# A chunked recurrence on one core: the 32 x 32 block inverse split into two halves of 16, masks back on VectorE, and a new table of lengths for the planner

## The chip, the cores and the metric

The kernel runs on one core of a Trainium2 chip. The metric is the device time of one execution in microseconds, as a median of several runs; lower is better. Engines are named as the profile does: PE is TensorE, DVE is VectorE, ACT is ScalarE, POOL is GpSimd, SP is SyncE, which here only issues transfers.

## What is computed

Three stages follow each other: a linear recurrence over 768 time steps in 4 x 8 heads of 40 dimensions, a mixture of eight experts with a capacity, and a dense feed-forward. The change lies in the first.

```python
for t in range(S):
    y[:, :, t] = np.einsum('bhd,bhde->bhe', rt, state)
    Sa = np.einsum('bhde,bhe->bhd', state, at)
    state_decay = state * wt[:, :, None, :] - np.einsum('bhd,bhe->bhde', Sa, bt)
    state = state_decay + np.einsum('bhd,bhe->bhde', vt, kt)
...
x = _moe_ref(x=x, **moe_kwargs)
return _moe2_ref(x=x, **moe2_kwargs)
```

## The kernel before

**Chunks.** Time is cut into 24 chunks of 32 steps. Within a chunk the dependence of a step on the steps before it is a lower triangular 32 x 32 matrix per head; its inverse turns 32 sequential updates into a few matmuls. Four chunks make one of six blocks (i = 0 to 5). A block has 8 steps of work, s = 8i to 8i + 7, each for one chunk and one half of the heads (hf).

**A step.** `kbt` transposes the keys (L531) into NI and Z, `chain` carries the state: X from AE and MV (L561), U from the inverse TB and X (L572), the new state MV from NI and MV (L589), scaled on VectorE (L593). `output` transposes MV into Z (L609), forms a product that is masked into RE (L622, L630), and sums the result into py (L641). After the last step of a chunk the router reads py.

**Preparation of a block.** `load` fetches, `prep` makes decays with two scans on VectorE (L370, L374), scales AE on VectorE or POOL (L377) and KB on POOL (L380). `gram` multiplies KB and AE (L407); one part of the product goes through the tile mab to DRAM (Md), the other is masked back into AE. `inverse` reads Md as Mu, one 32 x 32 matrix per partition, and eliminates column by column: a product into tmp (L470) and a subtraction from Tt (L472) for each of 30 columns, cut by rows into three ranges, two on VectorE (`VROW = (5, 10)`) and one on POOL. Tt goes to DRAM as Td and comes back as TB in the layout that `chain` needs.

**The first block.** `inverse_first` inverts two 16 x 16 halves on VectorE only, one instruction per half, column and operation (28 products, 28 subtractions). The off-diagonal quarter is then made on TensorE in `fix`: 32 small matmuls TB by Rt (L495), a masked copy to Wm (L497), 32 matmuls Wm by TB (L504), a copy back into TB. Rt is the transposed upper half, through DRAM as Tad.

**Masks.** With `GM = (0, 2)` half of AE's masks are a plain copy on ScalarE and a product on POOL (L431); the other half is one product on VectorE from PSUM (L422). `PM = 1` does the same for a quarter of RE's masks (L636 on POOL).

**What sets the order.** Nothing runs in the order of the code. `Sched` collects all operations of the recurrence with their lengths, dependences and due times (`when`, from START, STEP and the D constants), simulates the engines, picks the engine where several are allowed (`{'V': .., 'A': ..}`), and writes each engine's instructions in the order that it found. Where it expects TensorE to be idle it inserts small filler matmuls into py (L740). At run time each engine works through its list in that order, and so does SP's queue of transfers.

```python
NMV, NRE, NNI, NZ, NWT = 6, 7, 2, 3, 6
VROW = (5, 10)
START, STEP = 56.922, 7.975
DPREP, DINV, DOUT, DTURN = (-0.45, -0.74, 0.01, 1.52), (0.71, 9.76), 1.713, 0.084
EZ = 'A'
PM, ZM = 1, 0
GM = (0, 2)
```

Of the kernel before, what the change touches and what calls it, by code (L numbers as in the profile page):

```python
# [6 lines left out]
F32 = mybir.dt.float32  # L7
# [19 lines left out]
class Sched:  # L27
# [5 lines left out]
    AFTER = {'T': .25, 'V': .13, 'A': .18, 'P': .19, 'S': 0.}  # L33
# [198 lines left out]
    SLACK, PATIENCE, ALPHA = 0.021, 49.646, 0.109  # L232
# [3 lines left out]
SLACK0, LD0, LDS, PR0, PRS, LATEW, RV0, ZR0, ZRS, GR = 0.244, 0.0, 3.0, 18.956, 0.418, 0, 40.584, 52.618, 7.65, 1  # L236
# [39 lines left out]
def attention(ctx, tc, I, R, eng):  # L276
# [33 lines left out]
    TB4 = cp.tile([128, 2, 2, 8, 32], F32, name="TB")  # L310
    TBs = [TB4[:, m // 2, m % 2] for m in range(4)]
# [19 lines left out]
    Tad = dr.tile([32, 4, 16, 16], F32, name="Tad")  # L331
# [32 lines left out]
    def prep(n, h):  # L364
# [5 lines left out]
        op('V', .62, lambda E: E.tensor_tensor_scan(W, Bw[:, 0:528], d1, 0.0, ALU.mult, ALU.add), [('w', hf, h), 'd1'], ['W'])  # L370
        op('V', .07, lambda E: E.tensor_copy(WC, Ws[:, :, :, 32]), ['W'], [('WC', a, h)])
        op('V', .17, lambda E: E.reciprocal(rC, WC), [('WC', a, h)], [('rC', hf, h)])
        op(alu(512, EQ if n > 1 else 'V'), 0, lambda E: E.tensor_tensor(Qg, Ws[:, :, :, 0:32], rC.unsqueeze(3).broadcast_to([128, 2, 8, 32]), ALU.mult), ['W', ('rC', hf, h)], [('Q', hf, h)])
        op('V', .62, lambda E: E.tensor_tensor_scan(Bw[:, 527::-1], Bw[:, 527::-1], d1[:, ::-1], 1.0, ALU.mult, ALU.add), ['d1'], [('w', hf, h)])  # L374
# [7 lines left out]
    def turn(n):  # L382
        hf = n % 2
        Wo = Wts[n % NWT].rearrange("x (q j) e -> x q j e", j=2)
        for h in range(2):
# [5 lines left out]
            k = op('T', .44, f, [('Q', hf, x) for x in range(2)], [('ps', len(Q.ops))], ring='tr', act=1024)  # L391
# [5 lines left out]
    def gram(n, g):  # L397
        i, hf = divmod(n, 2)
        a, c8 = n % 4, 4 * (g // 2) + 2 * hf + g % 2
        AE, KB, mab = AEs[a], KBs[a], mabs[n % 2]  # L400
# [32 lines left out]
    def inverse_first(i):  # L433

        dma(Mu, Mds[i % 2].rearrange("c u t s -> (c u) t s"), 1 << 19, [('Md', i % 2, c) for c in range(8)], ['Mu'])
        op('P', 1.47, lambda E: (E.affine_select(Tt, Mu, [[-1, 32], [1, 32]], ALU.is_gt, 0.0, base=0, channel_multiplier=0),
                                 E.memset(Tt.rearrange("u a b -> u (a b)")[:, 0:1024:33], -1.0)), ['Mu'], [('Tt', x) for x in range(3)])
        for x in range(2):
            for k in range(1, 15):
                m, o, c = 15 - k, 16 * x, 16 * x + k  # L440
                tv = tmps[x][:, 0:k * m].rearrange("u (a b) -> u a b", b=m)
                d = alu(k * m, EI)
                tt = Tt[:, o:o + k, c + 1:o + 16]
                op(d, 0, lambda E, tv=tv, k=k, o=o, c=c, m=m: E.tensor_tensor(tv, Mu[:, c:c + 1, c + 1:o + 16].broadcast_to([128, k, m]), Tt[:, o:o + k, c:c + 1].broadcast_to([128, k, m]), ALU.mult),
                   ['Mu', ('Tt', x)], [('tmp', x)])
                op(d, 0, lambda E, tv=tv, tt=tt: E.tensor_tensor(tt, tt, tv, ALU.subtract), [('tmp', x)], [('Tt', x)])
        op(ev(256), 0, lambda E: copy(E, Ta, Tt[:, 0:16, 0:16].rearrange("u a b -> u b a")), [('Tt', 0)], ['Ta'])
        dma(Tds[i % 2].rearrange("u q s t -> (u q) s t"), Tt, 1 << 19, [('Tt', x) for x in range(3)], [('Td', i % 2)], QI)
# [5 lines left out]
    def inverse(i):  # L454
# [988 lines left out]
```

## Time and profile before

| what | us |
|---|---|
| median of 3 runs | 1141.11 (1140.74 to 1142.37) |
| the profiled execution | 1129.84 |
| its span, first to last instruction | 1128.1 |
| busy in the span: PE, DVE, ACT, POOL | 973.5, 791.4, 605.1, 484.1 |
| start of the first and end of the last py group of the recurrence | 107.4, 526 |

The shares of the whole span (PE 86%, DVE 70%) mix three stages. Up to about 530 us the recurrence runs, with DVE in the page's slices at nine tenths for most of the time up to 440 us; from 560 us on the experts and the feed-forward run, with PE at nine tenths throughout. The profiled execution is 1.0% below the median of the runs.

### The profile page before, as it was taken

What the parts mean: (1) busy time and instruction counts of PE and PEld (TensorE: products, weight loads), DVE (VectorE), ACT (ScalarE), POOL (GpSimd) and SP (SyncE); (2) the same over time, 40 slices, a digit from 0 to 9 for tenths busy, and PEclk for the clock granted to TensorE, in tenths of its full rate; (3) what the DMA queues carried; (4) which work ended last, traced back from release to release, by engine and by line L of the source; (5) the groups of instructions that cost most, each with busy time, mean ns of one, the idle gap of its engine ahead of it and who ended that gap; (6) DMA issues with size and microseconds to landing.
All of it is one profiled execution on the core that took longest, in us unless ns stands there. A gap on an engine that the chain in (4) does not pass through costs nothing.

```text
span 1128.1 us, 32070 instructions
## 1 busy us (share of the span) xinstructions
PE 973.5 (86%) x13099; PEld 863.8 (77%) x13099; DVE 791.4 (70%) x1857; ACT 605.1 (54%) x1426; POOL 484.1 (43%) x575
## 2 busy tenths in 40 slices
PE   4566787868877877997799999999999999999997
PEld 3555676756656666776688888999989999999997
DVE  8995878999999969534587778786755454444453
ACT  6135578757867778886444434444433333433343
POOL 7334435546545547112066556572948281010100
PEclk9867699979989889999799999999999999999999
DMA  7539575455454532430666666663211010000000
GB/s 214 197 77 253 136 198 155 114 128 156 142 124 132 147 76 69 99 97 20 219 212 193 193 176 207 211 175 106 71 36 48 24 24 24 1 24 1 24 13 15
DMA packets 134058, 127.80 MB, mean 113 GB/s; under 512 B 90768, under 2 KB 98576, under 8 KB 133904
## 3 DMA queue, kind: packets, MB, share of 16 engines
q1 hardware_dynamic: 131600, 117.79, 37.4%
q0 software_dynamic: 2304, 7.89, 1.9%
q8 instruction: 105, 1.72, 0.6%
q14 instruction: 49, 0.40, 0.1%
HBM read 101.48 MB, written 24.20 MB: 111 GB/s over the span
## 4 chain that ended last, share of the span: by engine, by line
PE 40%; DVE 19%; issue 9%; ACT 9%; DMA 4%; POOL 3%; SPq 1%; DVEq 0%; POOLq 0%; ACTq 0%
PE ph L997 16%; PE py L641 3%; PE oy L1204 3%; PE oy L1203 3%; PE oy L1202 3%; ACT Z L294 2%; DVE Tt L472 2%; DVE tmp L470 2%; DVE AE L377 2%; DMA wc<-cvm 2%; ACT NI L294 2%; ACT MV L294 2%; DVE RE L630 1%; DMA wa<-cvm 1%; PE tr L609 1%
## 5 line engine op out<-in xcount | busy, mean ns | idle before, releaser
L997 PE MATMUL ph<-xt,wq 128*128 128x512 f32 (+2 forms) x1408 | 311.8, 365 | 1.7 <-DVE xt L1038 1.6
L997 PEld LDWEIGHTS ph<-xt,wq 128*128 128x128 f32 x1408 | 248.5, 190 | 31.8 <-DVE xt L1038 2.8
L1182 DVE TENSOR_TENSOR gf<-gf,ph 128x512 f32<-128x512 f32 (+1 forms) x112 | 68.3, 610 | 97.6 <-ACT gf L1181 97.1
L1186 DVE TENSOR_TENSOR gl<-gf,gh 128x512 fp32r<-128x512 f32 (+1 forms) x112 | 77.9, 695 | 70.0 <-ACT gh L1185 70.0
L294 ACT COPY Z<-tr 40x512 f32<-40x512 f32 x192 | 101.1, 539 | 35.3 <-PE tr L609 32.5
L1181 ACT ACTIVATE gf<-ph 128x512 f32<-128x512 f32 (+1 forms) x112 | 60.0, 536 | 109.2 <-PE ph L997 106.9
L1212 POOL DMA_INDIRECT out_dram<-ob,gid x24 | 23.9, 994 | 218.5 <-ACT ob L1211 213.3
L1185 ACT CAST gh<-gf 128x512 fp32r<-128x512 f32 (+1 forms) x112 | 62.7, 559 | 96.5 <-DVE gf L1182 96.5
L1048 ACT ACTIVATE gh<-ph 128x448 fp32r<-128x448 f32 x64 | 34.9, 545 | 120.4 <-PE ph L997 120.4
L641 PE MATMUL py<-Z,RE 128*32 128x40 f32 x1536 | 77.4, 213 | 24.0 <-DVE RE L630 23.6
L641 PEld LDWEIGHTS py<-Z,RE 128*32 128x32 f32 x1536 | 67.4, 121 | 32.1 <-DVE RE L630 26.8
L1204 PE MATMUL oy<-wo,gl 128*128 128x320 f32 x288 | 89.3, 310 | 0.1
L1203 PE MATMUL oy<-wo,gh 128*128 128x320 f32 x288 | 89.0, 309 | 0.0
L1202 PE MATMUL oy<-wo,gh 128*128 128x320 f32 x288 | 88.9, 309 | 0.0
L1062 PE MATMUL y<-gh,wo 128*128 128x448 f32 x192 | 72.6, 378 | 5.6 <-DVE Y L1069 5.5
L472 DVE TENSOR_TENSOR Tt<-Tt,tmp 128x30 f32<-128x30 f32 (+19 forms) x275 | 76.3, 308 | 0.6
L609 PE MATMUL tr<-ident,MV 128*104 128x128 f32 x384 | 63.3, 298 | 10.3 <-DVE AE L422 4.9
L1065 PE MATMUL y<-gl,wo 128*128 128x448 f32 x192 | 70.4, 366 | 0.0
L470 DVE TENSOR_TENSOR tmp<-Mu,Tt 128x30 f32<-128x30 f32 (+19 forms) x275 | 69.0, 281 | 0.9
L589 PE MATMUL ch<-MV,NI 128*40 128x40 f32 x1472 | 54.8, 222 | 12.9 <-issue 5.3
L630 DVE TENSOR_TENSOR RE<-tr,maskP 64x128 f32<-64x128 f32 x144 | 41.3, 287 | 33.1 <-PE tr L622 17.4
L431 POOL TENSOR_TENSOR AE<-AE,maskP 32x256 f32<-32x256 f32 x40 | 32.0, 805 | 72.4 <-ACT AE L294 68.6
(181 smaller groups left out, 2297.7 us busy)
## 6 DMA issues: line engine op xcount, KB each, us to landing
KB<-in_kbT_dram SPq DMA_DIRECT2D x24, 512.0 KB, 6.0
RE<-in_rT_dram SPq DMA_DIRECT2D x48, 256.0 KB, 3.3
AE<-in_aT_dram SPq DMA_DIRECT2D x20, 512.0 KB, 6.2
raw<-in_wo_dram SPq DMA_DIRECT2D x16, 640.0 KB, 5.1
raw<-in_wqa_dram SPq DMA_DIRECT2D x16, 512.0 KB, 3.9
w<-in_wT_dram SPq DMA_DIRECT2D x24, 264.0 KB, 4.1
xs<-maskZ SPq DMA_DIRECT2D x8, 563.5 KB, 8.0
win<-xs SPq DMA_DIRECT2D x8, 563.5 KB, 8.0
```

What stands on the lines that cost most here:

```text
L294: (E.copy if E is A else E.tensor_copy)(o, i)
L470: op(e, d, lambda E, tv=tv, k=k, lo=lo, h=h, m=m: E.tensor_tensor(tv, Mu[:, k:k + 1, k + 1:].broadcast_to([128, h - lo, m]), Tt[:, lo:h, k ...
L472: op(e, d, lambda E, tv=tv, k=k, lo=lo, h=h: E.tensor_tensor(Tt[:, lo:h, k + 1:], Tt[:, lo:h, k + 1:], tv, ALU.subtract), [('tmp', x)], [t ...
L609: E.transpose(c['t'][0:104, q, :], MV[:, 4 * h + q], ident)
L641: E.matmul(py[32 * g:32 * g + 32, b, col:col + 40], RE[:, j, p, :], Z[:, p, ZC[j]:ZC[j] + 40], start=True, stop=True)
L997: T.matmul(ph, l, r, start=k == 0, stop=k == 7)
L1062: T.matmul(y[c], hi, gh, start=m == 0, stop=False)
L1065: T.matmul(y[c], hi, gl, start=False, stop=m == 7)
L1186: V.tensor_tensor(gl, gf, gh.bitcast(F32), ALU.subtract)
L1202: T.matmul(o, gh[:, sl], w[:, 0:320], start=m == 0, stop=False)
L1203: T.matmul(o, gh[:, sl], w[:, 320:640], start=False, stop=False)
L1204: T.matmul(o, gl[:, sl], w[:, 0:320], start=False, stop=m == 15)
```

## The change

- **The inverse.** `inverse_first` goes; every block is inverted by two halves of 16. Both halves are now in one instruction: Mu and Tt are 1056 elements wide and are seen as two diagonal 16 x 16 parts (Mb, Tb), so that a block has 14 products and 14 subtractions, all on VectorE. POOL only fills Tt.
- **The fix.** `back` loads TB and Rt, `fix` runs for each block on TensorE, due at DFIX = 6.599 steps after the start of the block before. TB has two buffers (TB4s), Tad too.
- **mab.** One copy of all 128 partitions in place of two of 32; four buffers; two transfers to Md per gram in place of one.
- **Masks and copies.** `GM = ()` and `PM = 0`: all masks are VectorE's. `EZ = 'AV'`: the copies Z from NI may go to VectorE.
- **The planner.** Most lengths and the AFTER constants are new (a scan 1.27 in place of 0.62, a mask 0.29 in place of 0.2, py 1.28), and so are SLACK, START, STEP and the D constants. All orders are new.

```diff
-    AFTER = {'T': .25, 'V': .13, 'A': .18, 'P': .19, 'S': 0.}
+    AFTER = {'T': .15, 'V': .08, 'A': .08, 'P': .15, 'S': 0.}
...
-VROW = (5, 10)
-EI = 'V'
...
-START, STEP = 56.922, 7.975
-DPREP, DINV, DOUT, DTURN = (-0.45, -0.74, 0.01, 1.52), (0.71, 9.76), 1.713, 0.084
+START, STEP = 66.553, 7.916
+DPREP, DINV, DOUT, DTURN, DFIX = (-1.52, -1.13, -0.18, 1.52), (2.13, 2.32), 1.968, 0.886, 6.599
...
-EZ = 'A'
-PM, ZM = 1, 0
-GM = (0, 2)
+EZ = 'AV'
+PM, ZM = 0, 0
+GM = ()
...
-        op('V', .62, lambda E: E.tensor_tensor_scan(W, Bw[:, 0:528], d1, 0.0, ALU.mult, ALU.add), [('w', hf, h), 'd1'], ['W'])
+        op('V', 1.27, lambda E: E.tensor_tensor_scan(W, Bw[:, 0:528], d1, 0.0, ALU.mult, ALU.add), [('w', hf, h), 'd1'], ['W'])
...
-        for par in range(2):
-            m = op(ev(256), 0, lambda E, par=par: copy(E, mo[:, :, :, par], c['t'][64 * par + 32:64 * par + 64]), [('ps', k)], [('mab', n % 2, g, par)], grp=('m', k))
-            Q.psum(k, m)
-        dma(Mds[i % 2][c8].rearrange('u t s -> t u s'), mo.rearrange('x p j a s -> x (p j a) s'), 131072, [('mab', n % 2, g, par) for par in range(2)], [('Md', i % 2, c8)])
+        m = op(ev(256), 0, lambda E: copy(E, mab, c['t']), [('ps', k)], [('mab', y)])
+        Q.psum(k, m)
+        Md = Mds[i % 2][c8].rearrange('(u a) t s -> a t u s', a=2)
+        for par in range(2):
+            dma(Md[par], mab[64 * par + 32:64 * par + 64].rearrange('x p j s -> x (p j) s'), 65536, [('mab', y)], [('Md', i % 2, c8, par)])
...
+        for k in range(1, 15):
+            m = 15 - k
+            if i:
+                when(8 * i - 8 + DINV[0] + (DINV[1] - DINV[0]) * k / 14)
+            tv = tmp[:, 0:2 * k * m].rearrange("u (x a b) -> u x a b", x=2, b=m)
+            tt = Tb[:, :, 0:k, k + 1:16]
+            d = .09 + 2 * k * m * .00104
+            op('V', d, lambda E, tv=tv, k=k, m=m: E.tensor_tensor(tv, Mb[:, :, k:k + 1, k + 1:16].broadcast_to([128, 2, k, m]), Tb[:, :, 0:k, k:k + 1].broadcast_to([128, 2, k, m]), ALU.mult),
+               ['Mu', 'Tt'], ['tmp'])
+            op('V', d, lambda E, tv=tv, tt=tt: E.tensor_tensor(tt, tt, tv, ALU.subtract), ['tmp'], ['Tt'])
...
             inverse(i + 1)
+            when(8 * i + DFIX)
+            back(i + 1)
+            for x in range(4):
+                when(8 * i + DFIX + .5 + x // 2 * 1.5)
+                fix(i + 1, x % 2, x // 2)
```

What the new table does to the order shows at three places. SP's queue at the start, between the first block's inverse (Td is written from Tt) and the loads TB and Rt that the first fix reads. Before:

```order
L343 DMA Td_183<-Tt_166 128x1024
L343 DMA Tad<-Ta 128x256
L343 DMA Md_182<-mab_159 32x16x32
L343 DMA w_126<-in_wT_dram 128x528
L343 DMA MV_119<-in_vt_dram 32x8x40
L343 DMA Md_182<-mab_158 32x16x32 x2
L343 DMA MV_119<-in_vt_dram 32x8x40
L343 DMA TB<-Td_183 128x16x32
L343 DMA Rt<-Tad 16x32x16 x4
```

After:

```order
L344 DMA Td_184<-Tt 128x1024
L344 DMA Tad_186<-Ta 128x256
L344 DMA Md_183<-mab_161 32x8x32 x2
L344 DMA Md_183<-mab_162 32x8x32 x2
L809 DMA xs<-maskZ 448x1x322 x2
L344 DMA TB_145<-Td_184 128x16x32
L344 DMA Rt<-Tad_186 16x32x16 x4
L344 DMA TB_145<-Td_184 128x16x32
```

The Md writes are those of the second block's grams and stand on both sides; the loads of w and MV have moved out, two of the writes of zeros to the experts' regions (xs) have moved in, and both TB loads stand together.

VectorE's queue where a later block is prepared: W and w are the scans, L422 and L424 masks on AE, L377 and L378 products on AE, L630 and L611 masks on RE, L593 and L574 the state. Before:

```order
L374 SCALAR_TENSOR_TENSOR w_126<-w_126,d_177 128x528
L370 SCALAR_TENSOR_TENSOR W<-w_127,d_177 128x528
L630 TENSOR_TENSOR RE_137<-tr,maskP 64x4x32 x2
L374 SCALAR_TENSOR_TENSOR w_127<-w_127,d_177 128x528
L593 TENSOR_TENSOR MV_118<-ch,WC_155 40x8x40 x2
L653 TENSOR_TENSOR xb_93<-py,Wt_150 128x320
L653 TENSOR_TENSOR xb_94<-py,Wt_150 128x160 x2
L422 TENSOR_TENSOR AE_129<-tr,maskP 32x4x32 x4
L371 COPY WC_153<-W 128x16
L377 TENSOR_TENSOR AE_128<-AE_128,Q_163 64x512
L372 RECIPROCAL rC_157<-WC_153 128x16
L377 TENSOR_TENSOR AE_128<-AE_128,Q_163 64x512
```

After:

```order
L371 SCALAR_TENSOR_TENSOR W<-w_127,d_178 128x528
L611 TENSOR_TENSOR RE_139<-tr,maskP 64x4x32 x4
L292 COPY Z_123<-NI_143 64x8x40
L375 SCALAR_TENSOR_TENSOR w_127<-w_127,d_178 128x528
L372 COPY WC_156<-W 128x16
L373 RECIPROCAL rC_158<-WC_156 128x16
L374 TENSOR_TENSOR Q_167<-W,rC_158 128x2x8x32
L574 TENSOR_TENSOR MV_119<-ch,WC_155 40x8x40 x2
L611 TENSOR_TENSOR RE_140<-tr,maskP 64x4x32
L378 TENSOR_TENSOR AE_131<-AE_131,Q_167 64x512
L611 TENSOR_TENSOR RE_140<-tr,maskP 64x4x32 x3
L371 SCALAR_TENSOR_TENSOR W<-w_126,d_178 128x528
```

Before, three scans, four masks and two AE products stand within one step; after, the same pieces are spread over the masks RE of two steps, and a copy Z stands among them.

TensorE's queue at the change of blocks (py is the end of a step, L572 or L553 the first reader of TB). Before:

```order
L572 MATMUL ch<-X_161,TB 32x40 x16
L622 MATMUL tr<-RE_136,Z_123 64x64 x8
L561 MATMUL ch<-MV_117,AE_130 32x40 x16
L531 MATMUL tr<-ident,KB_133 128x128 x4
L622 MATMUL tr<-RE_137,Z_124 64x64 x8
L641 MATMUL py<-Z_123,RE_136 32x40 x16
L407 MATMUL tr<-AE_129,KB_133 64x64 x8
```

After:

```order
L622 MATMUL py<-Z_123,RE_136 32x40 x16
L476 MATMUL tr<-Rt,TB_146 32x16 x64
L590 MATMUL tr<-ident,MV_121 104x128 x8
L570 MATMUL ch<-MV_122,NI_144 40x40 x16
L485 MATMUL tr<-TB_146,Wm_173 32x16 x32
L485 MATMUL tr<-TB_146,Wm_174 32x16 x32
L603 MATMUL tr<-RE_137,Z_124 64x64 x8
L409 MATMUL tr<-AE_128,KB_132 64x64 x16
L553 MATMUL ch<-X_163,TB_146 32x40 x16
```

The fix's groups (L476, L485) have come in between the groups of the block's last steps, seven groups ahead of the first one that reads the new TB.

## Rows read from the trace of the kernel before

**Rows 1.** Timeline of PE, py groups: start us, us, what, [idle before <-releaser].

```profile
285.59 1.33 PE L641 MATMUL py<-Z,RE 128*32 128x40 f32 x32
291.77 1.71 PE L641 MATMUL py<-Z,RE 128*32 128x40 f32 x32
...
332.49 1.44 PE L641 MATMUL py<-Z,RE 128*32 128x40 f32 x30 [0.36 <-DVE RE L630]
353.09 1.33 PE L641 MATMUL py<-Z,RE 128*32 128x40 f32 x32
```

**Rows 2.** Windows: stretch, its length, busy PE, PEld, DVE, ACT, POOL, PEclk, DMA, GB/s.

```profile
107.40:193.90 86.50, 69.56 (x1889) 59.02 (x1888) 72.76 (x218) 63.15 (x184) 41.81 (x56) 0.85 0.64 171
193.90:275.20 81.30, 62.59 (x1531) 51.78 (x1527) 76.77 (x234) 59.81 (x172) 43.15 (x71) 0.90 0.52 139
275.20:353.10 77.90, 61.43 (x1530) 50.77 (x1528) 73.89 (x228) 58.78 (x169) 40.86 (x67) 0.93 0.52 138
353.10:432.90 79.80, 62.55 (x1519) 52.72 (x1520) 65.17 (x225) 57.86 (x166) 41.32 (x70) 0.87 0.39 105
432.90:526.00 93.10, 82.97 (x2191) 69.72 (x2180) 49.65 (x206) 78.06 (x212) 24.87 (x52) 0.98 0.27 71
```

**Rows 3.** Windows for the tile Tt alone: length, busy DVE, ACT, POOL.

```profile
300.95:381.92 80.97, 26.89 (x111) 0.00 (x0) 16.11 (x42) 0.92 0.51 136
```

**Rows 4.** Groups by shape, 0 to 535 us, DVE: busy us, mean ns, idle.

```profile
L470 DVE TENSOR_TENSOR tmp<-Mu,Tt 128x5 f32<-128x5 f32 x10 | 9.5, 953 | 0.1
...
L470 DVE TENSOR_TENSOR tmp<-Mu,Tt 128x30 f32<-128x30 f32 x15 | 3.1, 217 | 0.1
...
L470 DVE TENSOR_TENSOR tmp<-Mu,Tt 128x110 f32<-128x110 f32 x5 | 1.5, 294 | 0.0
```

**Rows 5.** Groups of DVE in one block, 301 to 381 us.

```profile
L377 DVE TENSOR_TENSOR AE<-AE,Q 64x512 f32<-64x512 f32 x6 | 7.6, 1261 | 0.1
L593 DVE TENSOR_TENSOR MV<-ch,WC 40x320 f32<-40x320 f32 x15 | 7.3, 488 | 0.4
L630 DVE TENSOR_TENSOR RE<-tr,maskP 64x128 f32<-64x128 f32 x24 | 6.9, 287 | 2.9 <-ACT RE L294 2.3
...
L422 DVE TENSOR_TENSOR AE<-tr,maskP 32x128 f32<-32x128 f32 x16 | 4.6, 286 | 0.6 <-ACT AE L294 0.2
```

**Rows 6.** Groups of ACT in the same block.

```profile
L294 ACT COPY mab<-tr 32x256 f32<-32x256 f32 x16 | 5.8, 364 | 0.6 <-PE tr L407 0.4
L294 ACT COPY AE<-tr 32x128 f32<-32x128 f32 x16 | 4.0, 256 | 7.6 <-PE tr L407 6.3 <-DVE AE L422 1.1
```

**Rows 7.** Timeline of the first block's fix, second product.

```profile
87.63 0.91 PE L504 MATMUL tr<-TB,Wm 32*32 32x16 f32 x87 [0.21 <-ACT Wm L497]
```

**Rows 8.** Timeline of the start, 40 to 112 us.

```profile
41.14 1.37 POOL L436 TENSOR_SCALAR_AFFINE_SELECT Tt<-Mu 128x1024 f32<-128x1024 f32 x1 [10.39 <-DMA Mu<-Md]
...
54.02 0.23 DVE L444 TENSOR_TENSOR tmp<-Mu,Tt 128x14 f32<-128x14 f32 x2
...
64.72 0.33 SPq L343 DMA_DIRECT2D Td<-Tt  x1
...
73.87 0.47 SPq L343 DMA_DIRECT2D TB<-Td  x1
...
84.14 0.73 PE L495 MATMUL tr<-Rt,TB 16*32 16x16 f32 x64
...
91.26 1.32 PE L572 MATMUL ch<-X,TB 32*32 32x40 f32 x64
```

**Rows 9.** Timelines of DVE and POOL, 306 to 352 us.

```profile
319.27 0.69 DVE L377 TENSOR_TENSOR AE<-AE,Q 64x512 f32<-64x512 f32 x1
...
322.85 3.24 DVE L377 TENSOR_TENSOR AE<-AE,Q 64x512 f32<-64x512 f32 x1
...
323.37 2.17 POOL L380 TENSOR_TENSOR KB<-KB,w 128x1024 f32<-128x1024 f32 x1
```

**Rows 10.** Transfers by line: queue, kind, count, KB each, median us to landing.

```profile
TB<-Td SPq DMA_DIRECT2D x12, 256.0 KB, 4.0
```

More of the change, by code (lines that the diff above doesn't have):

```diff
@@ L309, in attention @@
     NIs = tiles(NNI, [128, 2, 8, 40], "NI")
-    TB4 = cp.tile([128, 2, 2, 8, 32], F32, name="TB")
-    TBs = [TB4[:, m // 2, m % 2] for m in range(4)]
+    TB4s = tiles(2, [128, 2, 2, 8, 32], "TB")
+    TBs = [t[:, m // 2, m % 2] for t in TB4s for m in range(4)]
     Wts = tiles(NWT, [128, 16, 40], "Wt")
@@ L330, in attention @@
     Tds = [dr.tile([32, 4, 32, 32], F32, name=f"Td{i}") for i in range(2)]
-    Tad = dr.tile([32, 4, 16, 16], F32, name="Tad")
+    Tads = [dr.tile([32, 4, 16, 16], F32, name=f"Tad{i}") for i in range(2)]
     def psum(ring='tr'):
@@ L399, in gram @@
         a, c8 = n % 4, 4 * (g // 2) + 2 * hf + g % 2
-        AE, KB, mab = AEs[a], KBs[a], mabs[n % 2]
+        y = 2 * (n % 2) + g % 2
+        AE, KB, mab = AEs[a], KBs[a], mabs[y]
         c = {}
@@ L431, in gram @@
                     op('P', .66, lambda E, t=t, o=o: E.tensor_tensor(t, t, maskP[o:o + 32].unsqueeze(1).broadcast_to([32, 8, 32]), ALU.mult), ['mask'], ak, sel=j == 1)
[L433 to L448, printed above, removed]
-        dma(Tad.rearrange("u q s t -> (u q) s t"), Ta, 1 << 17, ['Ta'], ['Tad'], QI)
     def when(s):
@@ new lines, in inverse, with back @@
+        op(ev(256, 'AV'), 0, lambda E: copy(E, Ta, Tt[:, 0:16, 0:16].rearrange("u a b -> u b a")), ['Tt'], ['Ta'])
+        dma(Tds[i % 2].rearrange("u q s t -> (u q) s t"), Tt, 1 << 19, ['Tt'], [('Td', i % 2)], QI)
+        dma(Tads[i % 2].rearrange("u q s t -> (u q) s t"), Ta, 1 << 17, ['Ta'], [('Tad', i % 2)], QI)
+    def back(i):
+        for gp in range(2):
+            dma(TB4s[i % 2][:, gp].rearrange("s h u t -> s (h u) t"), Tds[i % 2][16 * gp:16 * gp + 16].rearrange("u q s t -> (q s) u t"), 262144,
+                [('Td', i % 2)], [('TB', 4 * (i % 2) + 2 * gp + h) for h in range(2)], QI)
+        for q in range(4):
+            dma(R4[32 * q:32 * q + 16].rearrange("s m u t -> s (m u) t"), Tads[i % 2][:, q].rearrange("u s t -> s u t"), 80000, [('Tad', i % 2)], [('Rt', m, q) for m in range(4)], QI)
@@ L486, in fix @@
+    def fix(i, hf, gp):
         m = 2 * gp + hf
-        TB, Rt = TBs[m], Rts[m]
+        x = 4 * (i % 2) + m
+        TB, Rt = TBs[x], Rts[m]
         Wm = Wms[m % 2]
@@ L701, in attention @@
     when(0)
-    inverse_first(0)
+    inverse(0)
+    back(0)
+    for x in range(4):
+        when(2 * (x // 2) + x % 2)
+        fix(0, x % 2, x // 2)
     Q.slack = 0.
@@ L713, in attention @@
             inverse(i + 1)
+            when(8 * i + DFIX)
+            back(i + 1)
+            for x in range(4):
+                when(8 * i + DFIX + .5 + x // 2 * 1.5)
+                fix(i + 1, x % 2, x // 2)
             when(8 * i + DTURN)
@@ L720, in attention @@
             when(s)
-            if c % 4 == 0:
-                tbl(i, g // 2)
-                if s == 0:
-                    rtl()
-            if not i and g % 2 == 0:
-                fix(hf, g // 2)
             Q.since = RV0 if 2 <= s < 8 else 0.
```

93 lines of the change are left out of this document (35 added, 58 removed).

## Prediction, made before the change was timed

> **What bounds the kernel now.** I first cut the span where the program's own stages end. The last matmul group of a step writes py, so the starts of those groups are a clock of the recurrence. Two neighbouring ones lie 6.2 us apart in the quiet part of a block, and 20.6 us apart where the next block is prepared [rows 1]. The first such group starts at 107.4 us, the last step ends at 526, and everything behind it (router's tail, experts, feed-forward) is not touched by the change, so it can only move as a whole.
>
> Then the busy time of each engine between every eighth of these starts [rows 2]. A full block takes 81.3, 77.9 and 79.8 us, 79.7 in the mean. In the first two VectorE is busy 76.8 and 73.9 us, 94 to 95%; no other engine passes 79%. That makes VectorE the bound there. The third warns against stopping at that: VectorE is busy only 65.2 of 79.8 us, and the block is no shorter. Work that comes bunched (four masks, four AE products, a scan, all in the two long steps) lets one engine after another be the bound. The last row shows what a block costs without preparation: two blocks in 93.1 us, on a TensorE at clock 0.98.
>
> **What the change takes from VectorE.** All instructions on Tt and tmp keep VectorE busy for 26.9 us of a block, and POOL is counted beside it [rows 3]. They become 28 per block (14 products, 14 subtractions, from the loop's bounds). The new shapes have 28 to 112 elements a partition. The nearest rows are 0.217 us at 30 and 0.294 at 110 [rows 4]; at 0.26 in the mean that is 28 x 0.26 = 7.3 us. The lower bound is 28 x 0.2 = 5.6. The upper bound is the row of the same product at 5 elements: 0.953 us [rows 4], which no element count explains; 28 x 0.953 = 26.7. I take 7.3 because nearly all of the thirty-odd shapes in that view lie near the first two rows, and keep the other end for a rival.
>
> **What it gives VectorE.** With GM empty and PM zero, half of the masks come back: 16 on AE at 0.286 and 8 on RE at 0.287 us [rows 5], 6.9 us. In the new order 40 of the 96 copies Z from NI stand on VectorE, six in the block I counted; the nearest row is the MV product over 320 elements, 0.488 us [rows 5], so 2.9. One AE product fewer saves 1.3 [rows 5]. Sum: 75.3 - 26.9 + 7.3 + 6.9 + 2.9 - 1.3 = 64 us; the copies X that go to ScalarE (10 of 24 over the whole recurrence, four in the block I counted) take it to 63.
>
> **ScalarE and POOL.** ScalarE loses the 16 AE copies (4.0 us) and about half of the mab copies (16 of 0.364 become 8 over all 128 partitions; half is 2.9, nothing is the other end) [rows 6], and the RE and Z copies that moved. It gains eight small copies for the fix, some 2 us at the price of an AE copy. From 59 us it falls to about 51; it bounds nothing. POOL loses its third of the inverse and both mask loops; what stays are four KB products and three or four AE products.
>
> **TensorE.** The fix, done once before, is done for each block: 4 x 2 groups of 32 matmuls. In the first block a run of 64 took 0.73 us [rows 8], and one of 87 took 0.91 [rows 7]: 256 x 0.011 = 2.9 us per block, 15 us over five. The groups stand between the groups of the block's last steps, and in VectorE's order the inverse ends some four steps ahead of them, so its data has four steps (24 us at 6.2) for a write, SP's queue and a read that lands in 4.0 us [rows 10]. If that cover were gone, TensorE would stand there with the next block's first ch group queued behind it; the first block shows that price, 74 to 84 us [rows 8].
>
> The Trainium skill speaks against this part: "TensorEngine Tiling (Array Packing)", section Instruction Overhead, gives each matmul about 60 cycles whatever its size. At 2.4 GHz that would be an estimate of 256 x 0.025 = 6.4 us a block, 17 us more over five blocks if TensorE were the bound throughout, and the sum would end at 1097. The run of 64 in 0.73 us shows less than half of it, so the trace disagrees for these small tiles.
>
> **The queues.** SP gains 8 issues per block for Md (two half writes), one Tad, four Rt. With both TB buffers the two TB loads no longer wait for the last step of the block before. They stand together, and nothing waits behind them that the next step needs at once.
>
> **The start.** The first inverse begins at 54.0 us although POOL has filled Tt by 42.7, because five scans stand ahead of it in VectorE's order; Td leaves at 64.7, but TB is issued at 73.9 behind Md writes that wait for ScalarE; the fix comes at 84.1 and the first ch group that reads TB at 91.3 [rows 8]. In the new order six VectorE instructions stand there instead of thirteen, but some 25 others are mixed into the inverse (masks at 0.286, two scans, three AE products). Its 7 us and about 10 of theirs, from 44 on, end near 61, as before. The gain lies behind it: TB follows Td after two pairs of Md writes and two zero writes, and no gram other than that of its own block stands before the fix. Td at 61.5, TB at 66, landed at 71 to 73, fix done at 76, ch at 77: 14 us earlier, with the rest of block 1's preparation then done, as at 91 before. Bounds: 0, if Md and the zero writes hold TB as long as before; 22, if nothing does.
>
> **The blocks.** At the 94.5% that VectorE reached before, 63 us would need 67; at the 82% of the third block 77. The old 94.5% was reached because 110 small steps of the inverse filled every gap; the new order has a quarter of them, but spreads the scans and products over the whole block. I take 91%, nearer to the upper row, so 69 us. A second way: six quiet steps at 5.9 (6.2 now, where each waits behind inverse steps) make 35, the two long ones lose ScalarE's 7 us from their 40, giving 33; together 68. So 10.7 us for each of three blocks, 32. The first block, 86.5 us with 72.8 on VectorE and clock 0.85 [rows 2], loses the same VectorE work on a slower clock; I give it 12. The last two lose one inverse (22 us of VectorE, which is not their bound) and gain one fix: 3.
>
> **Sum.** 14 + 12 + 32 + 3 = 61 us. The profiled execution took 1129.84 us (span 1128.1), so one like it should show 1069. The median of the runs is 1141.11, 1.0% above; the same 61 us from it give **1080**.
>
> **The rivals.**
> Slower: POOL and VectorE get in each other's way. At 322.9 an AE product takes 3.24 us on VectorE while POOL's KB product runs from 323.4 to 325.5; the same shape took 0.69 at 319.3 [rows 9]. The new inverse steps read two SBUF tiles, too. If all 28 cost the 0.953 us of the 5-element row, VectorE needs 63 + 19.4 = 82 us, at 94.5% a block of 87: four blocks 7.4 longer each are 30, the start gains its 14 and pays 19 for its own 28 steps, so 1141 + 30 - 14 + 19 = 1176. With e us more per inverse the sum is 4 x ((63 + e) / 0.945 - 79.7) - 14 + e; it turns at e = 12.6, which is 0.71 us per step. Against it: POOL's busy time per block falls from 43 [rows 2] to about 20, and only one shape of some thirty shows the price.
> By "GPSIMD Engine Reference", section Key points, of the Trainium skill, the two engines share SBUF interfaces and collide where a VectorE instruction has two SBUF inputs; the 3.24 us row agrees, and the masks, with one input in PSUM, would be free of it.
>
> Less: the bunching stays. Engines wait in order for one another as in the third block, a block takes 75, the start gains 6, the first block 5: 6 + 5 + 14 = 25, 1116. For it: that third block. Against: the scans now stand two steps apart.
>
> More: everything interleaves. A block takes 63, the start gains 20, the first block 21, the last two 4: 95, 1046. For it: TensorE, busy 62 us at clock 0.90 to 0.93 [rows 2], needs with the 2.9 of the fix about 60 once the clock is nearly full, and 63 leaves it idle for 5%. Against: no stretch has all engines that dense.
>
> The same: the two effects cancel, three in a hundred.
>
> **Chances.** Forecast 50% (1062 to 1098), less 22% (1098 to 1130), more 20% (1036 to 1062), slower 5%, same 3%. Reaching into both neighbours until two in ten are left out: 1054 to 1114. A measurement of this kernel can tell about 0.2% from no change. Faster by more than that 92%, the same 3%, slower 5%.
>
> **What would show it.** Py starts 66 to 72 us apart over eight steps, and the first near 93. Instructions on Tt and tmp at 7 to 8 us of VectorE per block; if their mean is over 0.5 us, the slower rival is at work. VectorE 60 to 65 us a block, TensorE's clock above 0.9. Waits of the fix's first group for a DMA in every block would mean that its cover is gone. What would make the forecast wrong is a block above 74 or below 64.

## The result, and the profile after

The changed kernel takes **1148.05 us** (median of 5 runs, 1144.2 to 1149.82), the kernel before 1140.74 in the same series: a ratio of 1.0064 (1.0042 to 1.0086). It is 7 us slower; the forecast was 61 faster, and the range ended at 1114.

The profiled execution of after has a span of 1146.3 us, 18 above that of before; some 11 of these 18 come from before's profiled execution, which was that much faster than its median. From the page: span and instructions, the queue that loads instructions (packets, MB, share), and the chain that ended last.

```profile
span 1146.3 us, 37065 instructions
...
q8 instruction: 127, 2.08, 0.8%
...
PE 56%; DVE 14%; issue 13%; ACT 6%; DMA 5%; POOL 3%; SPq 3%; POOLq 0%; DVEq 0%; ACTq 0%
```

"Issue" is time in which an engine waited for nothing that the profile shows. The windows between every eighth py group, as [rows 2] has them of before:

```profile
108.10:208.50 100.40, 78.02 (x2321) 67.66 (x2318) 70.93 (x197) 51.88 (x147) 24.73 (x20) 0.83 0.53 136
208.50:285.90 77.40, 66.89 (x2081) 58.46 (x2080) 60.02 (x171) 51.22 (x145) 19.62 (x16) 0.91 0.54 140
285.90:364.60 78.70, 65.48 (x2057) 56.92 (x2056) 61.08 (x176) 50.22 (x142) 21.90 (x18) 0.91 0.53 140
364.60:443.90 79.30, 65.00 (x2039) 56.60 (x2039) 57.62 (x171) 49.15 (x139) 20.78 (x19) 0.89 0.45 120
443.90:542.00 98.10, 90.36 (x2714) 78.29 (x2714) 42.35 (x149) 73.98 (x203) 4.86 (x8) 0.91 0.29 72
sum 433.90, PE 365.75 PEld 317.93 DVE 292.00 ACT 276.44 POOL 91.90; mean PE 73.15 PEld 63.59 DVE 58.40 ACT 55.29 POOL 18.38
```

VectorE fell to 58 to 61 us in a full block, as forecast, and ScalarE and POOL too; yet the three full blocks take 78.5 us in the mean, where they took 79.7. The first block is 14 us longer, the last two 5. TensorE executes 2039 to 2081 matmuls in a full block, where it had 1519 to 1531. Its longest waits from 108 to 542 us (total, times, longest):

```profile
PE tr L485 <- issue: 11.4, 8, 2.3
PE tr L476 <- issue: 9.6, 8, 2.7
PE ch L553 <- issue: 8.7, 3, 5.6
PE tr L409 <- issue: 8.3, 6, 2.7
PE py L622 <- DVE RE L611: 4.6, 8, 1.1
```

Of before, the same view (107.4 to 526 us) begins otherwise:

```profile
PE py L641 <- DVE RE L630: 23.6, 22, 3.6
PE ch L589 <- ACT NI L294: 5.3, 12, 0.6
PE tr L609 <- DVE AE L422: 4.9, 3, 1.6
```

All gaps over 0.1 us, summed by what ended them: before, TensorE waited 65.7 us for data and 11.5 us with no cause shown ("unexplained" below); after, 14.4 and 52.7. So most of the waits that the change was to remove are gone, and others stand in their place. TensorE's own work over these stretches, before and after (columns as in [rows 2]):

```profile
107.40:526.00 418.60, 339.11 (x8629) 284.01 (x8629) 338.24 (x1107) 317.65 (x899) 192.01 (x312) 0.91 0.47 124
108.10:541.90 433.80, 365.64 (x11202) 317.83 (x11200) 292.00 (x860) 276.44 (x772) 91.90 (x81) 0.89 0.46 120
```

It was busy for 26 us more; the matmuls of the fix take 36.0 us of it after, and 3.2 before. One of the new waits, in the run of the fix near the end of block 2:

```profile
264.47 0.69 PE L409 MATMUL tr<-AE,KB 128*64 128x64 f32 x16
265.09 1.22 PE L476 MATMUL tr<-Rt,TB 16*32 16x16 f32 x120
269.01 0.31 PE L476 MATMUL tr<-Rt,TB 16*32 16x16 f32 x8 [2.70 <-issue]
269.25 1.14 PE L724 MATMUL py<-one 128*128 128x128 bf16 x9
```

TensorE stops in the middle of a group whose operands are all there. Counted through from the start, the stops lie at every 256th instruction of TensorE (a matmul and its weight load are two, and its waits for semaphores count as well): 52.3 of the 52.7 us, in 37 of 38 waits; before, 11.1 of 11.5. And each packet of q8 is 16 KB, 256 times 64 bytes. Worked out from the trace, the pages (256 instructions, at most 128 pairs of a weight load and a matmul) around that place, in us:

```
page entered | packet of the next page starts | last pair of the page | next page entered | wait
      241.22 |                         241.69 |                243.12 |            244.46 | 1.16
      244.46 |                         245.60 |                247.06 |            247.91 | 0.67
      247.91 |                         249.92 |                250.37 |            252.34 | 1.77
      252.34 |                         253.48 |                256.05 |            256.05 |
      256.05 |                         257.26 |                260.56 |            260.56 |
      260.56 |                         261.23 |                264.70 |            264.71 |
      264.71 |                         266.63 |                266.13 |            269.01 | 2.70
```

The packet of the next page starts after the page before it has been entered (84 of 88 from 108 to 542 us), 1.2 us later in the median, and where TensorE waited it went on 2.4 us (median) after that packet started. Of the 27 pages there that were executed in under 3.6 us (from entry to the start of the last pair), 25 end in a wait, 42 us in all; the other waits, 9 us, end longer pages whose packet started 1.8 us or more after they were entered. Before has one page as short as that. The Trainium skill, "Runtime: NRT & Kernel Launch", section Instruction fetch mechanics, describes blocks of 256 instructions, the next one fetched while the current one runs, and calls the crossing "mostly hidden". The trace agrees with the block and with the one page ahead; here the crossing is not hidden.

### The profile page after: what moved, and what is told of

Same layout as the page of the kernel before. It is cut to its first block, busy times and chain, and to the rows that moved or that the text cites. A ratio compares the mean times of both kernels' runs of the same rounds, so it can differ in the third digit from the quotient of the medians.

```text
span 1146.3 us, 37065 instructions
## 1 busy us (share of the span) xinstructions
PE 1009.7 (88%) x15918; PEld 906.1 (79%) x15918; DVE 735.6 (64%) x1571; ACT 552.8 (48%) x1264; POOL 378.5 (33%) x318
## 4 chain that ended last, share of the span: by engine, by line
PE 56%; DVE 14%; issue 13%; ACT 6%; DMA 5%; POOL 3%; SPq 3%; POOLq 0%; DVEq 0%; ACTq 0%
PE ph L981 17%; PE py L622 4%; PE oy L1188 3%; PE oy L1187 3%; PE oy L1186 3%; PE ch L570 2%; PE tr L590 2%; SPq L344 2%; PE tr L409 2%; ACT Z L292 2%; PE tr L512 2%; DVE tmp L450 2%; ACT NI L292 2%; PE y L1046 2%; PE tr L485 2%
## 5 line engine op out<-in xcount | busy, mean ns | idle before, releaser
L292 ACT COPY Z<-tr 40x512 f32<-40x512 f32 x192 | 98.3, 540 | 22.9 <-PE tr L590 21.2
L381 POOL TENSOR_TENSOR KB<-KB,w 128x1024 f32<-128x1024 f32 x21 | 47.2, 2245 | 159.4 <-PE py L622 34.4
L622 PE MATMUL py<-Z,RE 128*32 128x40 f32 x1536 | 73.7, 212 | 6.1 <-DVE RE L611 4.6
L611 DVE TENSOR_TENSOR RE<-tr,maskP 64x128 f32<-64x128 f32 x192 | 55.1, 287 | 34.3 <-PE tr L603 30.4
L622 PEld LDWEIGHTS py<-Z,RE 128*32 128x32 f32 x1536 | 65.8, 120 | 13.6 <-DVE RE L611 7.5
L574 DVE TENSOR_TENSOR MV<-ch,WC 40x320 f32<-40x320 f32 x92 | 44.9, 488 | 45.3 <-PE ch L570 43.7
L870 POOL DMA_INDIRECT xs<-xb,rii x24 | 25.6, 1068 | 142.0 <-DVE rii L860 95.2
L292 ACT COPY NI<-tr 64x160 f32<-64x160 f32 x192 | 55.1, 287 | 23.3 <-PE tr L512 20.0
L590 PE MATMUL tr<-ident,MV 128*104 128x128 f32 x384 | 60.2, 290 | 5.1 <-ACT NI L292 4.1
```

Of the source, the lines that this page charges most:

```text
L292: (E.copy if E is A else E.tensor_copy)(o, i)
L590: E.transpose(c['t'][0:104, q, :], MV[:, 4 * h + q], ident)
L622: E.matmul(py[32 * g:32 * g + 32, b, col:col + 40], RE[:, j, p, :], Z[:, p, ZC[j]:ZC[j] + 40], start=True, stop=True)
```

## Experiments

Three theories were set against each other. **Pages**: the fix's pairs use up TensorE's instructions faster than they are loaded. **Work**: TensorE's own busy time, at 0.0114 us a pair, is the cost. **Order**: the place of the fix in the order, and its chain of data, cost the gain.

**e5**, each matmul of the fix twice:

```diff
-                for q in range(4):
+                for q in (0, 1, 2, 3, 0, 1, 2, 3):
```

> The changed kernel, its planned order kept, with every matmul of the fix issued twice: 512 pairs more per block, 24 pages more in all, with the same result. Pages theory: 24 x 3.6 = 86 us, less the 14 us in which TensorE still waits for data: 65 to 90 us slower, 1213 to 1238. Work theory: 3072 pairs at 0.0114 us are 35 us at most: 1165 to 1183. Order theory: TensorE has slack around the fix, under 20 us slower: 1150 to 1168.

1231.43 us, 83 more than the changed kernel (ratio to before 1.081, 1.0713 to 1.0908). 3072 more pairs: 0.027 us each. In the recurrence TensorE's busy time rose by 47 us, its unexplained waits by 26 (to 79.0, 74.8 of them at page ends); those for data stayed at 14.4. The same place, where each page of the fix now ends in a wait:

```profile
292.51 1.19 PE L476 MATMUL tr<-Rt,TB 16*32 16x16 f32 x121
296.18 0.59 PE L476 MATMUL tr<-Rt,TB 16*32 16x16 f32 x46 [2.48 <-issue]
297.09 1.27 PE L476 MATMUL tr<-Rt,TB 16*32 16x16 f32 x82 [0.31 <-issue]
300.46 0.30 PE L476 MATMUL tr<-Rt,TB 16*32 16x16 f32 x7 [2.10 <-issue]
```

The time lies in the range of pages, and above those of work and order. But work is a large part of it. The recurrence as a whole:

```profile
115.30:622.30 507.00, 412.50 (x13957) 360.64 (x13956) 293.09 (x860) 276.69 (x772) 92.47 (x81) 0.83 0.39 104
```

Of the 73 us that it grew by, 38 are the matmuls of the fix themselves (73.7 us of TensorE in place of 36.0), 26 are unexplained waits, and 9 are the other 8450 matmuls, the same in both kernels: they took 343.2 us in place of 334.1, at a granted clock of 0.83 in place of 0.89 (a mean over time at 2.4 and at 1.2 GHz). So 0.027 us is the price of a pair with all three in it.

**e3 and e4**, the fix with a quarter of its pairs, e4 with fewer fillers as well:

```diff
-                for q in range(4):
-                    E.matmul(c['t'][32 * q:32 * q + 32, g], TB[32 * q:32 * q + 16, g], Rt[32 * q:32 * q + 16, g], start=True, stop=True)
+                E.matmul(b[:, 64 * g:64 * g + 64], TB[96:112, 0:4].rearrange("x g t -> x (g t)"), Rt[96:112, 0:4].rearrange("x g t -> x (g t)"), start=True, stop=True)
...
```

The second product is widened in the same way, and the copy back into TB writes zeros.

> The changed kernel, its planned order kept. Each group of 32 small matmuls of the fix (64 pairs in the trace, 0.73 us) is replaced by 8 matmuls over 128 columns of weights and 64 columns of data (16 pairs, about the same time on TensorE). The fix's result is not computed any more: the upper right quarters of the inverse are set to zero. 512 - 128 = 384 pairs fewer per block, 18 pages fewer in all, while every wait and copy stays. Pages theory: the stalls at the ends of the fix's pages go, and part of the others; 25 to 50 us faster, 1098 to 1123, and the waits of TensorE that no semaphore explains fall from 52 us to under 30. Work theory: same busy time, 1145 to 1151. Order theory: the chain from the inverse to the first group that reads it is as long as before, 1145 to 1151.

> The changed kernel, its planned order kept, with both edits: 258 transposes for the 715 fillers, and the fix's groups of 32 small matmuls replaced by 8 wide ones (the upper right quarters of the inverse are set to zero). About 78 pages up to the end of the recurrence, as many as the kernel before has. Pages theory: the stalls fall to about the 15 us of the kernel before, 35 to 55 us faster than the changed kernel, 1093 to 1113. Work theory and order theory: 1145 to 1151.

1160.39 and 1165.48 us (ratios to before 1.0157, 1.0084 to 1.023, and 1.0135, 1.002 to 1.0249), not faster than the changed kernel: the expected time was missed. In e3 TensorE's unexplained waits fell from 52.7 to 11.0 us, as pages say; but the wide matmuls kept TensorE busy for 0.13 us a pair, not the 0.046 that I had worked out, and groups on TB kept TensorE busy for 115.45 us in place of 60.13. The substitute was not neutral; these two runs say nothing on the sum.

**e6**, a better substitute: the same small tiles of weights, four matmuls of 128 columns for 32 of 16.

```diff
-            for g in range(8):
-                for q in range(4):
-                    E.matmul(c['t'][32 * q:32 * q + 32, g], TB[32 * q:32 * q + 16, g], Rt[32 * q:32 * q + 16, g], start=True, stop=True)
+            for q in range(4):
+                E.matmul(c['t'][32 * q:32 * q + 32], TB[32 * q:32 * q + 16, 0], Rt[32 * q:32 * q + 16], start=True, stop=True)
...
```

Here too the second product is changed in the same way, and the copy back writes zeros.

> The changed kernel, its planned order kept. Each group of 32 small matmuls of the fix (64 pairs, 16 columns each) becomes 4 small matmuls with the same tiles of weights and 128 columns each (8 pairs, the same columns in sum). The fix's result is not computed any more: the upper right quarters of the inverse are set to zero. 448 pairs fewer per block, 2688 or 21 pages in all. Run e5 measured 73 us for 2755 pairs more, 0.027 us each. Pages theory: up to 2688 x 0.027 = 72 us, less what waits for data take back: 40 to 72 us faster, 1076 to 1108; waits that no semaphore explains under 20 us. Work theory (0.0114 us of TensorE per pair): 31 us at most, 1117 to 1150. Order theory: 1145 to 1151.

**1088.51 us**, 60 less than the changed kernel (ratio to before 0.9547, 0.9504 to 0.9589). The windows:

```profile
100.40:185.00 84.60, 67.42 (x1706) 55.76 (x1703) 67.74 (x195) 51.42 (x148) 24.23 (x20) 0.92 0.69 181
185.00:256.20 71.20, 61.99 (x1633) 51.61 (x1632) 60.15 (x172) 50.69 (x144) 20.92 (x17) 0.98 0.61 160
256.20:325.70 69.50, 59.26 (x1609) 49.29 (x1608) 63.79 (x176) 50.91 (x146) 22.36 (x19) 1.00 0.62 164
325.70:396.10 70.40, 60.22 (x1590) 50.26 (x1591) 56.96 (x175) 47.94 (x137) 18.22 (x18) 0.93 0.48 122
396.10:484.80 88.70, 82.25 (x2266) 69.57 (x2266) 42.20 (x148) 72.70 (x201) 4.87 (x8) 1.00 0.31 78
sum 384.40, PE 331.14 PEld 276.48 DVE 290.84 ACT 273.67 POOL 90.60; mean PE 66.23 PEld 55.30 DVE 58.17 ACT 54.73 POOL 18.12
```

From the first py to the end of the recurrence 49.5 us went: busy TensorE 34.6, unexplained waits 26.3 (to 26.4, 19.2 of them at page ends), while waits for data came back by 11.3 (to 25.7). The longest waits are now for VectorE's masks, and behind them at page ends:

```profile
PE py L620 <- DVE RE L609: 9.9, 15, 1.7
PE ch L551 <- issue: 7.4, 7, 2.5
```

Of the 34.6 us of busy time only 18.0 are the fix's. The other 16.6 are the same 8450 other matmuls, 317.5 us in place of 334.1, at a granted clock of 0.97 in place of 0.89. In the changed kernel's wait of 2.70 us shown above, the clock fell to 1.2 GHz at 268.0 us, and it rose again at 278.3. Whether the waits lower the clock or the small tiles of the fix do was not separated: in e3, with 11.0 us of unexplained waits, it stood at 0.91.

A full block takes 70.4 us in the mean: 69 was forecast. With its pairs nearly gone, the fix's chain of groups, copies and transfers costs little: order falls a second time. Pages account for 26 of the 49.5 us, the fix's own time for 18 and the other matmuls for 17, and VectorE's masks and other data take 11 back.

**e7**, the fix's number of pairs put into the kernel before:

```diff
                     E.matmul(py[32 * g:32 * g + 32, b, col:col + 40], RE[:, j, p, :], Z[:, p, ZC[j]:ZC[j] + 40], start=True, stop=True)
+            for x in range(8):
+                for q in range(4):
+                    E.matmul(py[32 * q:32 * q + 32, 2, 320 + 16 * x:336 + 16 * x], ident[32 * q:32 * q + 16, 32 * q:32 * q + 32], ident[32 * q:32 * q + 16, 0:16], start=True, stop=True)
```

> The kernel before, its planned order kept, with 32 small matmuls (64 pairs, 16 rows by 32 columns of weights, 16 columns of data, as in the fix) added behind each of the 48 groups that write py; nothing reads what they write. 512 pairs more per block, as many as the changed kernel's fix has, 24 pages in all. Pages theory: 0.027 us per pair, 82 us, of which TensorE's waits for data (66 us before) can take a part: 40 to 82 us slower, 1181 to 1223. Work theory: 0.0114 us per pair, 35 us at most, hidden where TensorE waits: 1141 to 1176.

1182.57 us (ratio 1.0347, 1.028 to 1.0414): 40 more than before in the same series, at the near edge of pages. 3072 pairs cost 0.013 us each here, since TensorE's waits for data gave up 32 of their 66 us; its unexplained waits rose from 11.5 to 47.0, 41.8 of them at page ends. L644 is the added line:

```profile
PE py L644 <- issue: 21.7, 18, 3.7
PE ch L572 <- issue: 6.4, 7, 2.0
PE py L641 <- DVE RE L630: 4.9, 6, 1.9
```

**e1**, the fillers as 258 transposes of f32 for 715 matmuls of bf16:

```diff
-            for _ in range(self.fill.get(i, 0)):
+            for _ in range(round(self.fill.get(i, 0) / 2.7)):
...
-    Q.emit(lambda: T.matmul(py[:, 2, 320:448], R.one, R.one, start=True, stop=True))
+    Q.emit(lambda: T.transpose(py[:, 2, 320:448], ident, ident))
```

> The changed kernel, its planned order kept, with TensorE's 715 fillers (matmuls of 128 bf16 columns, 0.055 us) replaced by 258 transposes of 128 f32 columns (some 0.15 us each): about the same time on TensorE, 457 fewer matmul-with-load pairs, or 3.6 pages of 128 pairs. Pages theory (TensorE's instructions come in pages of 256, and the next page is fetched only after the one before it has been entered, so a page takes at least 1.2 + 2.4 = 3.6 us): up to 3.6 x 3.6 = 13 us faster, 1135 to 1144. Work theory (TensorE's own busy time is what was added): no change, 1146 to 1150. Order theory (the fix's place in the order and its data chain cost the gain): no change, 1146 to 1150.

1147.83 us, no change (ratio to before 1.0056, 1.0024 to 1.0089), against my 4 to 13. Of the 457 pairs fewer only 160 lie in the recurrence behind its first py, and the unexplained waits there did not fall (56.6). So the fillers are not shown to matter; 160 pairs are too few for this run to tell more.

**e9**, a planner that knows pages:

```diff
+    def pages(self, t, end, n):
+        left = 128 - self.seen
+        self.seen += n
+        if n < left:
+            return end
+        self.seen -= 128
+        at = t + (end - t) * left / n
+        on = max(at, self.page[0] + self.PAGE)
+        self.page[0] = on
+        return end + on - at
...
-                end = self.array(work, t, d, o['act'] or 1650. * d)
+                end = self.pages(t, self.array(work, t, d, o['act'] or 1650. * d), o['n'])
```

> The changed kernel with a planner that knows pages: each TensorE operation has its number of pairs, and a page of 128 pairs takes at least 3.6 us; the planner's constants (due times, slack, choice of engines for two copies, fillers) are set anew for the earliest end under that rule. Pages theory: by the planner's own reckoning the recurrence ends 29 us earlier than in the changed kernel's order under the same rule; 15 to 35 us faster, 1113 to 1133, and the waits that no semaphore explains fall from 52 us to under 35. Work theory and order theory: another order of the same work, of either sign, 1130 to 1170.

1154.2 us (ratio 1.0108, 1.0083 to 1.0132): slower still. The unexplained waits fell to 39.6 us, not to under 35 as expected, and waits for data rose to 36.6, 19.6 of them for RE's masks. This other order of as many pairs did not pay; that none would is not shown.

**e10, e11, e12**, no fix behind the first block. The whole 32 x 32 inverse is made on VectorE in 30 x 2 steps:

```diff
+        if i:
+            for k in range(1, 31):
+                m = 31 - k
...
+                op('V', d, lambda E, tv=tv, k=k, m=m: E.tensor_tensor(tv, Mu[:, k:k + 1, k + 1:32].broadcast_to([128, k, m]), Tt[:, 0:k, k:k + 1].broadcast_to([128, k, m]), ALU.mult), ['Mu', 'Tt'], ['tmp'] + [('Rt', x, q) for x in range(4) for q in range(4)] * (i == 1 and k == 1))
+                op('V', d, lambda E, tv=tv, tt=tt: E.tensor_tensor(tt, tt, tv, ALU.subtract), ['tmp'], ['Tt'])
...
-                fix(i + 1, x % 2, x // 2)
```

> The changed kernel without its fix in blocks 2 to 6: their inverse is made whole on VectorE, in 30 x 2 steps (20 us by 0.165 us and 1 ns per element a step, where the two halves take 7.3), nothing else than the due times of its steps is set anew (spread over steps 2 to 4 of a block). 512 pairs fewer in each of five blocks, 20 pages. Pages theory: 2560 x 0.027 = 69 us less on TensorE, and VectorE has the room (60 us busy of a 78 us block, 73 then): 30 to 60 us faster than the changed kernel, 1088 to 1118, TensorE's waits that no semaphore explains under 25 us. Rival, VectorE is the bound again: 73 us at the 94.5 per cent that it reached before are 77 us a block, so no faster than the kernel before, 1130 to 1150.

> As e10, with half of the masks on POOL as in the kernel before and all copies Z on ScalarE, the planner knowing pages of 3.6 us, and its due times and slack set anew for the earliest end. VectorE's load falls from 73 to some 64 us per block. Pages theory: planned end 416 us where the changed kernel's order had 504 under the same rule and took 541 on the chip; scaled by that ratio 450, so 80 to 100 us before the changed kernel's: 1050 to 1070. Rival, POOL and VectorE in each other's way: POOL's mask products stretch VectorE's 60 steps and the gain of the moved masks is lost, 1090 to 1125.

> As e10, all masks on VectorE, the planner knowing pages of 3.6 us, and its due times and slack set anew. Pages theory: planned end 430 us, scaled as for e11 461, so 1060 to 1085. Rival, VectorE is the bound: 77 us a block, 1130 to 1150.

1129.67, 1121.13 and **1112.91 us** (ratios to before 0.9831, 0.9787 and 0.9719, the last 0.9671 to 0.9766). All three beat both kernels, and all three miss the pages theory's times. Full blocks of e10 and then of e12:

```profile
193.70:272.30 78.60, 69.48 (x1756) 59.57 (x1754) 72.40 (x206) 50.08 (x141) 23.25 (x19) 0.98 0.55 143
272.30:354.20 81.90, 67.33 (x1720) 58.84 (x1718) 74.82 (x201) 49.53 (x139) 23.33 (x20) 0.96 0.49 133
```

```profile
180.70:258.90 78.20, 64.71 (x1649) 55.61 (x1649) 72.59 (x199) 49.80 (x142) 21.70 (x17) 0.96 0.52 141
258.90:338.70 79.80, 65.39 (x1674) 56.46 (x1674) 73.74 (x197) 51.14 (x144) 21.93 (x20) 0.98 0.52 138
```

The unexplained waits are 10.9 us in e10, but VectorE is at 91 to 93% of these blocks, which are no shorter, as the rival of e10 and e12 said of a VectorE that is the bound again. By the time, e10 is just under that rival's range, and e12 lies between both ranges. In e10 TensorE did not get all that the fix gave back, either: the planner put 940 fillers into the recurrence behind the first py, where the changed kernel has 249. e11 lies in the range of its own rival (POOL's masks stretch VectorE's steps); an instruction on Tt took 0.40 us there and 0.37 in e12, so that stretch is small, and what holds e11 stays open. What they gain lies in the first block (82 and 77 us, where the changed kernel takes 100) and in the last two.

**e13 and e14**, the eight zero writes to xs 30 planned us later, in the changed kernel and in e12:

```diff
+            if self.ops[i]['xfer'] == 1.6:
+                late.append((t + LATE, i, e))
+                continue
```

> The changed kernel, its planned order kept, but for the eight zero writes to xs (0.56 MB each), which are issued 30 planned us later, behind the loads of the first TB and Rt instead of ahead of and among them. Queue theory of the start (SP's queue and the transfers in it hold the first fix: TB issued at 72.9 and 80.2 us, first group that reads it at 85): the two TB issues move up by 2 to 5 us, the first py by 3 to 8 us, and the time by as much, 1140 to 1145. Rival, the start is held by the inverse (ended at 67 us) and the transfers' own latency: within 2 us of the changed kernel, 1146 to 1150.

> e12 with the zero writes to xs issued 30 planned us later, as in e13. Queue theory: in e12 the first zero writes follow the first loads of TB anyway, so little is left, 0 to 4 us faster, 1108 to 1114. Rival: the writes then meet the second block's loads and Md writes in SP's queue, 1113 to 1125.

1142.88 (ratio to before 1.0022, 0.9995 to 1.0049) and 1118.08 us. SP's queue in e13:

```profile
71.03 0.40 SPq L352 DMA_DIRECT2D TB<-Td  x1
71.53 2.87 SPq L352 DMA_DIRECT2D Rt<-Tad  x4
74.44 0.49 SPq L352 DMA_DIRECT2D TB<-Td  x1
```

The second TB load moved from 80.2 to 74.4 us, the first py from 108.1 to 102.7, and the time by 5, with intervals of the ratio that just overlap. But the first group that reads TB moved by 2 us only (85.1 to 83.1), and so did the scan that waits for its decays (96.8 to 94.9). Most of the rest at the first py is a wait of 3.1 us at a page end, which lies ahead of it in the changed kernel; here one of 2.8 us lies behind it. In e1, whose queue is that of the changed kernel, the first py came at 102.0 as well, with no gain in time. So the queue is worth some 2 us at the start, and its theory holds in part; what the other 3 us of the time are is not shown. In e12, where both TB loads already stood ahead of the writes (70.0 and 74.6 against 87.6), moving them gained nothing: 5 us more, in the range of the rival.

## Why the prediction was wrong

**VectorE: right.** The inverse's instructions cost 8.6 us a block (7.3 forecast, a little above its 7 to 8), with the windows of Tt alone:

```profile
208.50:285.90 77.40, 8.28 (x27) 0.91 0.54 140
285.90:364.60 78.70, 8.81 (x28) 0.91 0.53 140
364.60:443.90 79.30, 8.76 (x29) 0.89 0.45 120
```

VectorE has 58 to 61 us of a full block (63), ScalarE 49 to 51 (51), POOL 20 to 22 (about 20). The fix's first groups waited 0.6 us for a DMA in all from 108 on: its cover held. And e6 shows the block that these terms give, 70.4.

**TensorE: the step that failed**, "256 x 0.011 = 2.9 us per block, 15 us over five", a term that the sum took for covered, because VectorE was held to be the bound. It failed in three ways.

- The count: a group of 32 matmuls in the program is 64 in the trace (each f32 matmul runs as two), and the run of 64 in [rows 8] was one group, not two. A block has 512 pairs, not 256, and in a full block the fix kept TensorE busy for 6.0 to 6.9 us.
- The price: 0.011 us, read from runs that fit into one page, is TensorE's own time alone, which came out near it (0.0127). In a long run a page of 128 pairs takes some 1.2 + 2.4 us, 0.028 a pair, and the difference is waiting: 7.9, 10.0 and 11.9 us at page ends in the three full blocks, where before had 0.6 to 1.9.
- The bound: busy time alone said that TensorE had room, since the loading of instructions shows in no engine's busy share. In the full blocks TensorE is now busy for 65.8 us, waits 9.9 without a cause shown and 2.6 for data: 78.3 of 78.5.

Over the recurrence 33 us of the fix and 41 of unexplained waits came, and 51 of waits for data went. At the 0.027 of e5, 2560 pairs are 69 us in place of 15, more than the 61 forecast; e6, which takes 2688 pairs away, gives back 60, 17 of these from the other matmuls, which ran at a higher clock.

The rule that I had set aside, the Trainium skill, "TensorEngine Tiling (Array Packing)", section Instruction Overhead, is no better an account: 0.025 us, my estimate from its 60 cycles, is twice the 0.0127 that a pair of the fix took of TensorE. That the 0.022 to 0.027 in all come near it is owed to page ends and clock.

**The start: 14 us forecast, none gained.** The inverse ended at 67.1 us, not at 61. At three places in it VectorE met POOL's products (a copy of 0.15 us took 2.2, an AE product of 0.69 took 1.7), some 5 us in all; at 57.8 a step of 0.27 us took 2.14:

```profile
57.76 2.14 DVE L450 TENSOR_TENSOR tmp<-Mu,Tt 128x108 f32<-128x108 f32 x1
```

while POOL had begun a KB product:

```profile
57.58 2.19 POOL L381 TENSOR_TENSOR KB<-KB,w 128x1024 f32<-128x1024 f32 x1 [6.28 <-DVE w L375]
```

That is the slower rival's mechanism, at twice the 0.953 us that it named, but at few steps. Then SP's queue, where I had TB at 66:

```profile
69.56 1.91 SPq L344 DMA_DIRECT2D Md<-mab  x4
71.52 1.33 SPq L809 DMA_DIRECT2D xs<-maskZ  x2
72.89 1.55 SPq L344 DMA_DIRECT2D TB<-Td  x1
74.48 5.67 SPq L344 DMA_DIRECT2D Rt<-Tad  x4
80.20 0.49 SPq L344 DMA_DIRECT2D TB<-Td  x1
```

The first ch group that reads TB came at 85.1, 6 us earlier than in [rows 8]; page waits of 2.3 and 3.1 us (ended at 88.0 and 105.3; before had one of 1.7 there) and a scan whose decays SP issued only at 92 took the 6 back before the first py. Without the zero writes (e13) the groups on TB come 2 us earlier; the rest was not tried.

**The first block**, 12 us forecast, 14 lost: 17.1 us of unexplained waits stand there, where before had 5.7, and the fix has 9.5 us of TensorE, where before had 3.2; waits for data fell by 6. In e6, which still has 12.7 us of unexplained waits there, it takes 84.6, 2 us less than before; why not 74.5 stays open.

**The rivals.** None named this mechanism. "Less" and "more" moved around the same bound, and "slower" was looked for on VectorE. The paragraph on "more" had TensorE at 60 us of a 63 us block and left it at that.

## What to carry to other kernels

Cost work that moves to TensorE by instructions as well as by busy time: count the matmuls in the trace, not in the program, and compare the pace of the stretch that they move to with the pace at which pages come (here 128 pairs in 3.6 us). A price read from a short run holds for short runs. Compare the granted clock, too, before a difference in busy time is put down to the instructions that were added or removed. When an engine's idle time has no releaser in the profile, look at which instruction it stops, and at the instruction queue's packets.

## What the runs showed of the hardware

- In the changed kernel TensorE's waits with no cause shown stood at every 256th instruction: 37 of 38 waits and 52.3 us in the recurrence, 5.6 us the longest. 25 of the 27 pages executed in under 3.6 us ended so.
- The packet of the next page started 1.2 us (median) after a page was entered, up to 5.4 us in the changed kernel and 6.0 before; what delays it was not settled.
- TensorE itself ran the fix's pairs at 0.0127 us each (6.5 us busy for 512 in a block). With page ends and clock, a pair more or less changed the time by 0.022 to 0.027 us where TensorE was the bound (e6, e5), and by 0.013 where it waited for data (e7).
- The same 8450 other matmuls of the recurrence took 343.2, 334.1 and 317.5 us at granted clocks of 0.83 (e5), 0.89 (the changed kernel) and 0.97 (e6).
- A matmul of f32 with 128 columns of weights and 64 of data kept TensorE busy for 0.128 us a pair with 16 rows and 0.139 with 128 rows (e3, clock 0.91), ten times a pair of the fix.
